# A fused windowed-attention and gated feed-forward kernel: wo loaded in three row parts, the third half's attention placed over its whole stage, cross-pair sums in two operations each

## The chip, the cores and the metric

The kernel runs on one core of a Trainium2 chip. The metric is device time in microseconds. One execution was also taken by the hardware profiler; its page and trace are the source of every duration below. Engine names are those of the profile: PE is TensorE, PEld its weight loads, DVE VectorE, ACT ScalarE, POOL GpSimd and SP the engine that only issues DMAs; POOL and ACT issue DMAs as well. L607 means line 607 of the kernel before.

## What is computed

The inputs are q, k and v of 4 batches, 8 heads, 768 positions and 64 elements per head, and three weight matrices. Attention sees, for each query, the first 8 positions and the 96 positions up to its own, with a bias that falls with distance at a slope of each head's own. The heads side by side make 3072 tokens of 512 elements, which a gated feed-forward layer takes to 1536 and back.

```python
is_global = pos[None, :] < n_global            # 8
is_local  = (rel >= 0) & (rel < n_local)       # 96
scores = q @ k.T / sqrt(D) - slopes * dist     # dist = n_local for far globals
a = softmax(where(is_global | is_local, scores, -1e9))
x = (a @ v) with heads side by side            # 3072 x 512
out = (relu(x @ w_gate) * (x @ w_val)) @ w_out
```

## The kernel before, in words

**Halves and stages.** The work is cut into 8 halves of 384 queries, numbered s = 0 to 7: half s is the first or the second half of the positions of batch s // 2. Each half gets attention (scores, exponentials, a multiplication by a mask, the product with v, division by the sums) and then, under the same number c, the feed-forward layer. TensorE works on the layer of half c while the attention of half c + 1 is placed between its matmuls, and while POOL and SP prepare the keys and queries of half c + 2. The order on each engine is the order in which the program emits instructions; `weave` (L682) emits a list of feed-forward blocks and puts other pieces behind the block at which their share of the list, between 0 and 1, is reached. `spread(items, first, last)` (L677) gives pieces evenly spaced shares.

**The feed-forward layer.** `ffn_pieces` (L598) makes, for each of 12 blocks of 128 hidden rows, a gate block and a value block of four 128x384 matmuls each (L607). ScalarE takes relu of the gate (L614), VectorE multiplies it with the value into `ht` (L620). PSUM has three banks for these ("ff") and five for attention ("x"), so the third block after a given one needs its bank back. Then come the output products with `wo_sb`: plain ones (`outp`, L622, four parts of three row blocks each, L627), or in pairs of 128 tokens by a scheme with seven half-width products instead of eight (`winograd`, L512, matmuls L549), which needs sums of `ht` (`add`, L529 to L535, VectorE) and sums of quarters of `wo_sb` (`wo_sum`, L828, VectorE). From half 4 on, the third 128 tokens of two neighbouring halves make such a pair too; its sums (`add3` in the change, buffers "sums3") run in the stages of halves 5 and 7, behind value blocks 1, 6 and 7, on all six row blocks at once. Results leave through `osb` tiles: copies on ScalarE (L566, L578, L581, L584), additions on VectorE (L569, L574, L588, L589), and DMAs on SP.

**Attention of halves 2 to 7.** `attention_pieces` (L493) gives, for each of four pairs of heads, three score pieces (eight matmuls L397 into four x banks, exponentials L406 on ScalarE, masks L359 on VectorE), two products with v (L427, logarithms of the sums L436 and the exponential that inverts them, L441, on ScalarE), and a norm (L446, VectorE). Empty pieces, two each time for half 2, one for the others, space them.

**Keys and queries.** Loads on SP (L113) bring them in, POOL casts them (`piece_cast`, L361, eight per half), SP transposes them by three DMA transposes (`piece_x`, L367), and `piece_order` (L372) copies the keys of each pair into order, three copies per pair: on POOL, and for pairs 2 and 3 of half 2 on ScalarE.

**The stage that the change touches most** is the last of three `weave` calls for halves 0 and 1: the last 4 hidden blocks of each (16 gate and value blocks), then plain products of half 0 (12 blocks) and the outputs of half 1 (11 blocks), 39 blocks in all, with the attention of half 2, the preparation of half 3 and the sums of `wo_sb` placed into it. Before it POOL has been given, in this order: the load of `wo_sb` (L155, one DMA of all 12 row blocks, in `loads`, L798), fills, the loads of v for half 2, the casts of half 2, with a one-element copy `held` ahead of the last cast that reads the last row block of `wo_sb` and so makes POOL wait for it, two key copies, and the loads for half 3.

Of the kernel before, what the change touches and what calls it, by code (L numbers as in the profile page):

```python
# [15 lines left out]
def kernel(  # L16
# [12 lines left out]
    nc = tc.nc  # L29
# [4 lines left out]
    DM = H * D  # L34
    DFF = moe_w_gate.shape[1]
    N_DC = DM // 128
    N_FC = DFF // 128
# [58 lines left out]
    wo_sb = const.tile([128, N_FC, DM], BF16)  # L96
# [3 lines left out]
    def w_of(t, dc, fc):  # L100
        f = fc % GW
        return t[fc // GW][:, dc, f * 128 : (f + 1) * 128]
# [15 lines left out]
    def v_dst(b, r0, r1, j):  # L118
        t = vbuf[b % 2][r0:r1, j, D:]
        return t.rearrange("p (h z) -> p h z", z=2 * D)[:, :, 0:D]  # L120
# [5 lines left out]
    def spread_v_globals(b, j0=1, j1=NT):  # L126
        if b == 0:
            for j in range(j0, j1):
                nc.sync.dma_start(out=v_dst(b, 0, NG, j), in_=v_dst(b, 0, NG, 0))
        else:  # L130
            t = vbuf[b % 2]
            nc.sync.dma_start(out=t[0:NG, j0:j1, :], in_=t[0:NG, 0:1, :].to_broadcast(
                [NG, j1 - j0, (2 * H + 1) * D]))
# [19 lines left out]

    def load_w(dst, src, f0, f1):
        nc.gpsimd.dma_start(out=dst, in_=src[:, f0:f1].rearrange("(c p) f -> p c f", p=128))  # L155

    def load_w_group(i):
        load_w(wg[i], moe_w_gate, i * GW * 128, (i + 1) * GW * 128)
        load_w(wv[i], moe_w_val, i * GW * 128, (i + 1) * GW * 128)
# [201 lines left out]
    def piece_cast(s, p, i):  # L361
        of = (ks_of, qs_of)[i]
        nc.gpsimd.tensor_copy(  # L363
            kqc[:, :, i].rearrange("t n (h d) -> t h n d", d=D)[:, 2 * p : 2 * p + 2],
            of[s][:, 2 * p : 2 * p + 2, :].rearrange("t e (n d) -> t e n d", n=NN))

    def piece_x(s, n):  # L367
        nc.sync.dma_start_transpose(
            out=kqT[s % 2].rearrange("d i p t -> d (i p) t")[:, :, n * 128 : (n + 1) * 128],
            in_=kqc[:, n].rearrange("t i z -> t (i z)"))  # L370

    def piece_order(s, p):  # L372
        b, half = divmod(s, 2)
        copy = nc.scalar.copy if s == 2 and p >= 2 else nc.gpsimd.tensor_copy
        put_keys(copy, copy, kT[b % 2][p], kNb[s % 2][:, p], half)

    def early_pieces(s):
        out = [(0.0, lambda p=p, i=i: piece_cast(s, p, i)) for i in range(2) for p in range(HP)]
        out += [(0.0, lambda n=n: piece_x(s, n)) for n in range(NN)]
        out += [(0.0, lambda p=p: piece_order(s, p)) for p in range(HP)]  # L380
        return out
# [111 lines left out]
    def attention_pieces(s):  # L493
        QK = lambda p: [(0.15, lambda g=g: piece_qk(s, p, g)) for g in range(3)]
        AV = lambda p: [(0.29, lambda e=e: piece_av(s, p, e)) for e in range(2)]
        N = lambda p: [(0.0, lambda: piece_norm(s, p))]
        g = QK(3)
        a = AV(2)
        gap = [(0.0, lambda: None)] * (2 if s == 2 else 1)
        return (QK(0) + QK(1) + AV(0) + N(0) + gap + QK(2) + AV(1) + N(1) + gap  # L500
                + g[0:1] + a[0:1] + g[1:2] + a[1:2] + g[2:3] + N(2) + AV(3) + N(3))

# [95 lines left out]
    def ffn_pieces(c):  # L598
        ht = ht_pool.tile([128, N_FC, QH], BF16, name="ht")
        st = {}  # L600

        def product(w, key, fc, d0, d1):
            key = key, fc
            if d0 == 0 and key not in st:
                st[key] = psum["ff"].tile([128, 512], FP32, name="ff_ps")
            for dc in range(d0, d1):
                nc.tensor.matmul(st[key][:, 0:QH], lhsT=w_of(w, dc, fc), rhs=xT_of[c][:, dc, :],  # L607
                                 start=(dc == 0), stop=(dc == N_DC - 1))

        def gate(fc, d0=0):  # L610
            product(wg, "g", fc, d0, N_DC)
            psg = st["g", fc]
            gr = gr_pool.tile([128, QH], BF16, name="grelu")
            nc.scalar.activation(gr, psg[:, 0:QH], AF.Relu, bias=0.0, scale=1.0)  # L614
            st["gr", fc] = gr

        def val(fc, d0=0):
            product(wv, "v", fc, d0, N_DC)
            psv = st["v", fc]
            nc.vector.tensor_tensor(ht[:, fc, :], psv[:, 0:QH], st["gr", fc], op=ALU.mult)  # L620

        def outp(n, part):  # L622
            if part == 0:
                st["o"] = psum["ff"].tile([128, 512], FP32, name="ff_ps")
            ps2 = st["o"]
            for fc in range(part * N_FC // 4, (part + 1) * N_FC // 4):
                nc.tensor.matmul(ps2, lhsT=ht[:, fc, n * 128 : (n + 1) * 128],  # L627
                                 rhs=wo_sb[:, fc, :],
                                 start=(fc == 0), stop=(fc == N_FC - 1))
            if part == 3:  # L630
                osb = late["osb"].tile([128, DM], FP32, name="osb")
                nc.scalar.copy(osb, ps2)
                nc.sync.dma_start(out=out_v[c, n], in_=osb)

        def begin():
            two = psum["s"].tile([128, 2, 512], FP32, name="s_ps")
            st["g", 1], st["v", 1] = two[:, 0], two[:, 1]
            for d0, d1 in ((0, 2), (2, N_DC - 1)):
                for key, w in (("g", wg), ("v", wv)):
                    for fc in range(2):  # L640
                        product(w, key, fc, d0, d1)

        plain = range(NN) if c < 1 else () if c - c % 2 in PAIRED else (NN - 1,)
        add, products = winograd([(c, ht, 0), (c, ht, 1)], "sums", (1, 5, 6, 4, 7, 2, 3) if c == NHALF - 1 else
                                 (1, 2, 5, 6, 4, 3, 7) if c in PAIRED else (1, 5, 4, 6, 2, 3, 7))
        behind = {2: [lambda: add(3, 0, 3)], 7 if c == 2 else 5: [lambda: add(3, 3, 6)], 8: [lambda: add(1, 0, 3)],
                  9: [lambda: add(2, 0, 3)], 10: [lambda: add(4, 0, 3)]}
        rest = tuple(lambda j=j: add(j, 3, 6) for j in (1, 2, 4))
        if c in PAIRED:
            third_of[c] = ht  # L650
        elif c - 1 in PAIRED:
            add3, products3 = winograd([(c, ht, NN - 1), (c - 1, third_of[c - 1], NN - 1)], "sums3",
                                       (1, 5, 4, 6, 2, 3, 7))
            behind.update({1: [lambda: add3(1)], 6: [lambda: add3(2)], 7: [lambda: add3(3)]})
            rest = (lambda: add3(4),) + rest

        def val_and_sums(fc):
            val(fc)
            for f in behind.get(fc, ()):
                f()  # L660

        begin_of[c] = (begin, lambda fc=0: gate(fc, N_DC - 1), lambda fc=0: val(fc, N_DC - 1))
        f1 = []
        for fc in range(N_FC):
            f1.append((0.65, lambda fc=fc: gate(fc)))
            f1.append((0.65, lambda fc=fc: (val if c < 1 else val_and_sums)(fc)))
        f2 = [(0.65, lambda n=n, part=part: outp(n, part))
              for n in plain for part in range(4)]
        if c >= 1:
            f2 += (products3 if c - 1 in PAIRED else []) + products  # L670
            places = (2, 3, 5) if plain else (0, 1, 2) if c in PAIRED else (0, 1, 2, 3)
            for at, f in list(zip(places, rest))[::-1]:
                f2.insert(at, (0.0, f))
        return f1, f2


    def spread(items, first, last):  # L677

        n = len(items)
        return [(first + (i + 0.5) / n * (last - first), f) for i, (_, f) in enumerate(items)]  # L680
# [116 lines left out]

    def loads():  # L798
        load_w_group(2)
        load_w(wo_sb, moe_w_out, 0, DM)  # L800
        Z()

    more = {"K0": lambda: load_qk_after(2), "S20": loads}
# [1 line left out]
    for f in ("m0 g0 g1 v0 m3 K3 m2 g2 m1 v1 K2 v2 S30 K0 S31 K1 S21 g3 S20 v3 S01 A3 N3 S00 S11 "  # L805
              "g6 g7 A2 S10 g4 v7 A0 N2 v4 v6 A1 N0 N1 g5 v5").split():
        i = int(f[1])
# [34 lines left out]
    E = [f for _, f in early_pieces(2)]  # L842
    casts, xs, order_k = E[0:8], E[8:11], E[11:15]
    held = rc_pool.tile([1, 1], BF16, name="held")
    for f in (*casts[:7], lambda: nc.gpsimd.tensor_copy(held, wo_sb[0:1, N_FC - 1, 0:1]),
              casts[7], *xs, lambda: spread_v_globals(1), *order_k[:2]):
        f()
    load_qk_after(3, nc.gpsimd)
    load_v_half(3)
    weave(f1_1[G[0]])  # L850
    weave(f1_1[G[1]], [(0.1 + 0.12 * j, lambda j=j: fill_ones(nc.vector, 0, j)) for j in range(NT)])
    weave(f1_0[G[2]] + f1_1[G[2]] + f2_0 + f2_1,
          [(0.33, order_k[2]), (0.38, order_k[3])],
          spread(attention_pieces(2), 0.375, 0.925), spread(early_pieces(3), 0.58, 0.88),
          spread([(0.0, lambda j=j, part=part: wo_sum(j, part)) for j in (1, 3, 2, 4) for part in range(2)],
                 0.1, 0.74))

    ahead = {}
    for c in range(2, NHALF):
# [53 lines left out]
```

## Time and profile before

| | |
|---|---|
| median of three runs | 240.01 us (239.62 to 240.66) |
| profiled execution | 240.08 us, of which 238.3 are the span from the first instruction to the last |
| clock granted to TensorE | 1.0 over the whole span |
| matmuls, gate and value (L607) | 768 of 128x384 in all, 326 ns each as recorded |
| half-width products (L549) | 324 of 128x256, 272 to 273 ns each as recorded |
| plain products (L627) | 68 of 128x512, 379 ns each |
| relu (L614), ht (L620) | 491 ns, 555 ns |
| sums of ht (L535), 384 and 768 wide | 370 to 374 ns, 546 to 627 ns |
| load of wo_sb | one DMA of 1536 KB, 19.0 us from issue to landing |
| DMA transposes | 18 on SP |

A row of the profile gives the line, the engine, the operation, what it writes and reads, how often, the busy time and the mean duration. Recorded durations of matmuls overlap, so a full TensorE shows in the distance between starts. What stands in brackets behind an instruction in the timeline is the idle time of its engine just before it and what ended that.

### The profile page before, as it was taken

The numbers are of one execution on the slowest core, as the hardware profiler recorded it, in microseconds if no ns is written. First come the engines' busy times: TensorE is split into PE (matmuls) and PEld (weight loads), VectorE is DVE, ScalarE is ACT, GpSimd is POOL, SyncE is SP. The second block draws the span as 40 slices with busy tenths as digits, with TensorE's granted clock in tenths as the row PEclk, the third lists the DMA queues.
The fourth block names the chain that finished last, engine by engine and source line by source line (L and its number), as shares of the span: only waits on it lengthen the run. The fifth ranks groups of instructions, "written<-read, shape, count | busy, mean of one in ns | idle before, by whom it ended". The sixth has DMA issues, their size and how long they took to land.

```text
span 238.3 us, 5431 instructions
## 1 busy us (share of the span) xinstructions
PE 231.7 (97%) x1977; PEld 150.1 (63%) x1981; DVE 171.8 (72%) x456; ACT 156.1 (66%) x358; POOL 89.5 (38%) x204
## 2 busy tenths in 40 slices
PE   7899999999999999999999999999999999999994
PEld 3655565655557566666667666856588666766683
DVE  7775965768756778666787677868985786955752
ACT  5896983438767777757777678557686578634330
POOL 6795897007433860903275042723350000000000
PEclk9999999999999999999999999999999999999999
DMA  6999999993996897098519955198432200020022
GB/s 208 183 170 174 241 263 213 191 162 47 286 205 124 260 194 135 10 183 259 101 33 111 236 155 111 25 157 249 78 59 88 90 1 0 4 88 0 3 80 97
DMA packets 70515, 31.42 MB, mean 132 GB/s; under 512 B 47176, under 2 KB 67400, under 8 KB 70488
## 3 DMA queue, kind: packets, MB, share of 16 engines
q0 software_dynamic: 32800, 8.71, 36.0%
q1 hardware_dynamic: 36472, 21.45, 34.3%
q10 hardware_dynamic: 1216, 0.92, 1.2%
q8 instruction: 15, 0.25, 0.4%
q14 instruction: 12, 0.10, 0.1%
HBM read 28.41 MB, written 6.29 MB: 146 GB/s over the span
## 4 chain that ended last, share of the span: by engine, by line
PE 86%; DMA 7%; DVE 2%; POOL 1%; ACT 1%; issue 1%; DVEq 0%
PE ff_ps L607 50%; PE ff_ps L549 12%; DMA wg<-in_moe_w_gate_dram 7%; PE ff_ps L627 7%; PE x_ps L427 6%; PE x_ps L549 5%; PE x_ps L397 4%; PE t_ps L700 1%; PE t_ps L459 1%; POOL kq L737 1%; PE t_ps L272 1%; DVE es L359 0%; DVE ht L620 0%; ACT lnd L436 0%; DVE osb L574 0%
## 5 line engine op out<-in xcount | busy, mean ns | idle before, releaser
L607 PE MATMUL ff_ps<-xT,wg 128*128 128x384 bf16 x380 | 77.7, 326 | 0.4 <-DMA wg<-in_moe_w_gate_dram 0.2
L607 PE MATMUL ff_ps<-xT,wv 128*128 128x384 bf16 x380 | 77.6, 326 | 0.2 <-DVE osb L574 0.2
L614 ACT ACTIVATE grelu<-ff_ps 128x384 bf16<-128x384 f32 x95 | 46.5, 491 | 45.1 <-PE ff_ps L607 23.2
L620 DVE TENSOR_TENSOR ht<-ff_ps,grelu 128x384 bf16<-128x384 f32 x95 | 52.7, 555 | 30.2 <-PE ff_ps L607 19.1
L607 PEld LDWEIGHTS <-wg 128*128 128x128 bf16 x384 | 36.1, 98 | 23.6 <-issue 1.0
L607 PEld LDWEIGHTS <-wv 128*128 128x128 bf16 x384 | 35.8, 98 | 23.3 <-issue 0.5
L406 ACT ACTIVATE es<-x_ps 128x360 bf16<-128x360 f32 (+2 forms) x96 | 35.6, 447 | 3.2 <-PE x_ps L397 3.2
L359 DVE TENSOR_TENSOR es<-es,m_all 128x432 bf16<-128x432 bf16 (+4 forms) x108 | 29.7, 325 | 6.0 <-ACT es L406 5.8
L446 DVE TENSOR_TENSOR xT<-x_ps,rcp 64x384 bf16<-64x384 f32 x48 | 26.6, 554 | 9.2 <-ACT rcp L441 8.4
L436 ACT ACTIVATE lnd<-x_ps 64x384 f32<-64x384 f32 x48 | 23.3, 485 | 10.9 <-PE x_ps L427 10.2
L363 POOL CAST kqc<-ks 128x384 bf16<-128x384 f32 x24 | 12.1, 554 | 31.7 <-DMA ks<-in_k_dram 31.7
L549 PEld LDWEIGHTS <-s 128*128 128x128 bf16 x216 | 21.1, 98 | 2.9 <-issue 0.4
L549 PE MATMUL ff_ps<-t,s 128*128 128x256 bf16 x162 | 21.6, 272 | 0.3 <-ACT osb L584 0.3
L427 PE MATMUL x_ps<-es,vbuf 128*128 128x216 bf16 (+4 forms) x216 | 21.8, 225 | 0.0
L137 POOL DMA_DIRECT2D vbuf<-in_v_dram x25 | 21.6, 881 | 0.3 <-DVE s L535 0.3
L427 PEld LDWEIGHTS <-vbuf 128*128 128x128 bf16 x216 | 15.8, 97 | 6.8
L627 PE MATMUL ff_ps<-wo_sb,ht 128*128 128x512 bf16 x68 | 17.6, 379 | 0.2
L549 PEld LDWEIGHTS <-ht 128*128 128x128 bf16 x162 | 15.5, 98 | 2.3
L263 POOL COPY kT<-kqT 128x240 bf16<-128x240 bf16 x16 | 7.1, 442 | 22.2 <-DMA kqT<-kqc 19.2
L363 POOL CAST kqc<-qs 128x384 bf16<-128x384 f32 x24 | 12.1, 541 | 6.2 <-DMA qs<-in_q_dram 6.2
L535 DVE TENSOR_TENSOR s<-ht 128x384 bf16<-128x384 bf16 (+1 forms) x32 | 12.5, 392 | 0.8
L441 ACT ACTIVATE rcp<-lnd 128x384 f32<-128x384 f32 x24 | 12.6, 524 | 0.8
(118 smaller groups left out, 247.0 us busy)
## 6 DMA issues: line engine op xcount, KB each, us to landing
out_dram<-osb SPq DMA_DIRECT2D x23, 256.0 KB, 2.4
ks<-in_k_dram SPq DMA_DIRECT2D x6, 768.0 KB, 6.2
qs<-in_q_dram SPq DMA_DIRECT2D x6, 768.0 KB, 11.5
vbuf<-in_v_dram POOLq DMA_DIRECT2D x21, 120.0 KB, 7.7
wo_sb<-in_moe_w_out_dram POOLq DMA_DIRECT2D x1, 1536.0 KB, 19.0
wg<-in_moe_w_gate_dram POOLq DMA_DIRECT2D x2, 512.0 KB, 9.8
wv<-in_moe_w_val_dram POOLq DMA_DIRECT2D x2, 512.0 KB, 11.0
wg<-in_moe_w_gate_dram POOLq DMA_DIRECT2D x2, 256.0 KB, 5.8
```

The source lines that it names most:

```text
L137: nc.gpsimd.dma_start(out=v_dst(b, NG + r0, NG + r0 + n, j), in_=v[b, :, KT * j + r0 : KT * j + r0 + n, :].rearrange("h p d -> p h d"))
L359: nc.vector.tensor_mul(for_all, for_all, mk)
L363: nc.gpsimd.tensor_copy(kqc[:, :, i].rearrange("t n (h d) -> t h n d", d=D)[:, 2 * p : 2 * p + 2], of[s][:, 2 * p : 2 * p + 2, :].rearrang ...
L406: nc.scalar.activation(es[:, e, 0:c], banks[e][:, 0:c], AF.Exp, bias=0.0, scale=scale)
L427: nc.tensor.matmul(av3[:, :, a : a + w], lhsT=vb[:, j, z0 : z0 + 128], rhs=es[:, e, c : c + NN * w].rearrange("k (n p) -> k n p", n=NN), s ...
L436: nc.scalar.activation(ln[o0 : o0 + 64], av[d0 : d0 + 64, 0:QH], AF.Ln, bias=0.0, scale=1.0)
L446: nc.vector.tensor_tensor(xT_of[s][r, p, :], av_of[s, p, e][r, 0:QH], av_of[s, p, "r"][r], op=ALU.mult)
L549: nc.tensor.matmul(st[key][:, 0:D2], lhsT=left(i), rhs=right(i), start=start and i == 0, stop=i == N2 - 1, skip_group_check=not start)
L607: nc.tensor.matmul(st[key][:, 0:QH], lhsT=w_of(w, dc, fc), rhs=xT_of[c][:, dc, :], start=(dc == 0), stop=(dc == N_DC - 1))
L614: nc.scalar.activation(gr, psg[:, 0:QH], AF.Relu, bias=0.0, scale=1.0)
L620: nc.vector.tensor_tensor(ht[:, fc, :], psv[:, 0:QH], st["gr", fc], op=ALU.mult)
L627: nc.tensor.matmul(ps2, lhsT=ht[:, fc, n * 128 : (n + 1) * 128], rhs=wo_sb[:, fc, :], start=(fc == 0), stop=(fc == N_FC - 1))
```

## The change

- `wo_sb` is loaded in three DMAs of four row blocks each. The first takes the old place. The second and the third are issued on POOL behind the key copies of pairs 0 and 1 of half 2, so behind that half's transposes; `held` follows them instead of standing ahead of the last cast.
- Half 2's attention is placed from 0.125 to 0.88 of its stage, before from 0.375 to 0.925, with one empty piece each time instead of two; the key copies of pairs 2 and 3 go from 0.33 and 0.38 to 0.2 and 0.25, the sums of `wo_sb` from 0.1 to 0.74 to 0.36 to 0.76.
- In the stages of halves 5 and 7, the second and third cross-pair sums are made in two operations of three row blocks each, behind value blocks 3 and 6, and 4 and 7.

```diff
+    def load_wo(i):
+        f = N_FC // 3
+        nc.gpsimd.dma_start(out=wo_sb[:, i * f : (i + 1) * f], in_=moe_w_out[i * f * 128 : (i + 1) * f * 128].rearrange(
+            "(c p) f -> p c f", p=128))
...
-        gap = [(0.0, lambda: None)] * (2 if s == 2 else 1)
+        gap = [(0.0, lambda: None)]
...
-            behind.update({1: [lambda: add3(1)], 6: [lambda: add3(2)], 7: [lambda: add3(3)]})
+            behind[1] = [lambda: add3(1)]
+            for fc, j, i in ((3, 2, 0), (4, 3, 0), (6, 2, 3), (7, 3, 3)):
+                behind[fc] = [lambda j=j, i=i: add3(j, i, i + 3)]
...
-        load_w(wo_sb, moe_w_out, 0, DM)
+        load_wo(0)
...
-    for f in (*casts[:7], lambda: nc.gpsimd.tensor_copy(held, wo_sb[0:1, N_FC - 1, 0:1]),
-              casts[7], *xs, lambda: spread_v_globals(1), *order_k[:2]):
+    for f in (*casts, *xs, lambda: spread_v_globals(1), order_k[0], lambda: load_wo(1), order_k[1],
+              lambda: load_wo(2), lambda: nc.gpsimd.tensor_copy(held, wo_sb[0:1, N_FC - 1, 0:1])):
         f()
...
-          [(0.33, order_k[2]), (0.38, order_k[3])],
-          spread(attention_pieces(2), 0.375, 0.925), spread(early_pieces(3), 0.58, 0.88),
+          [(0.2, order_k[2]), (0.25, order_k[3])],
+          spread(attention_pieces(2), 0.125, 0.88), spread(early_pieces(3), 0.58, 0.88),
           spread([(0.0, lambda j=j, part=part: wo_sum(j, part)) for j in (1, 3, 2, 4) for part in range(2)],
-                 0.1, 0.74))
+                 0.36, 0.76))
```

## The prediction

> **What bounds the kernel now.** I read the page first, then the waits, then the timeline around each place where TensorE stood still.
>
> The page's busy shares and its chain:
>
> ```profile
> PE 231.7 (97%) x1977; PEld 150.1 (63%) x1981; DVE 171.8 (72%) x456; ACT 156.1 (66%) x358; POOL 89.5 (38%) x204
> ...
> PE 86%; DMA 7%; DVE 2%; POOL 1%; ACT 1%; issue 1%; DVEq 0%
> ```
>
> TensorE sets the end. The change removes no matmul, so it can win only TensorE idle time. Busy time hides small holes, because matmuls overlap; I took them from start times: four 384-column matmuls occupy 0.65 us (gate starts 46.26, value starts 46.91), six 256-column ones 0.655. The waits name who ended the three holes after 28 us that the change can reach:
>
> ```profile
> PE ff_ps L549 <- ACT osb L584: 0.3, 1, 0.3
> PE ff_ps L607 <- DVE osb L574: 0.2, 1, 0.2
> PE ff_ps L607 <- DVE ht L620: 0.2, 1, 0.2
> ```
>
> The first two stand at the end of the third half's stage:
>
> ```profile
> 74.77 0.52 ACT L441 ACTIVATE rcp<-lnd 128x384 f32<-128x384 f32 x1
> 75.20 0.35 ACT L584 COPY osb<-ff_ps 128x256 f32<-128x256 f32 x1
> 75.33 1.14 DVE L446 TENSOR_TENSOR xT<-x_ps,rcp 64x384 bf16<-64x384 f32 x2 [1.24 <-ACT rcp L441]
> 75.60 0.81 PE L549 MATMUL ff_ps<-t,s 128*128 128x256 bf16 x6 [0.26 <-ACT osb L584]
> ...
> 76.84 0.41 DVE L574 TENSOR_TENSOR osb<-ff_ps,osb 128x256 f32<-128x256 f32 x1
> ...
> 77.31 0.81 PE L607 MATMUL ff_ps<-xT,wv 128*128 128x384 bf16 x4 [0.24 <-DVE osb L574]
> ```
>
> The product block before 75.60 started at 74.53, so the next was due at 75.18: 0.42 lost behind the copy L584, which queued on ScalarE behind the last pair's logarithms and rcp. The gate block started at 76.25, the next was due at 76.90 and came at 77.31: 0.41 lost behind L574, itself behind the last pair's norms. The third hole is in piece 5's stage:
>
> ```profile
> 167.52 0.71 DVE L535 TENSOR_TENSOR s<-s,ht 128x768 bf16<-128x768 bf16 x1
> 168.15 1.59 DVE L359 TENSOR_TENSOR es<-es,m_all 128x432 bf16<-128x432 bf16 x4
> 169.66 0.55 DVE L620 TENSOR_TENSOR ht<-ff_ps,grelu 128x384 bf16<-128x384 f32 x1
> ...
> 170.26 0.81 PE L607 MATMUL ff_ps<-xT,wg 128*128 128x384 bf16 x4 [0.17 <-DVE ht L620]
> ```
>
> The block before began at 169.27, so 169.92 was due: 0.34 lost behind a 768-wide sum and four masks. Together 1.17 us, 0.49% of 240.08: the most that this change can win.
>
> **The change, part by part.** Sums are against the profiled run, 240.08 us (span 238.3 and 1.8 around it); the median is 240.01, 0.07 lower.
>
> *Cross-pair sums in halves.* One 768-wide sum behind value 6 and one behind value 7 become 384-wide halves behind values 3, 4, 6, 7. In the chain above the sum occupied VectorE 0.63 (167.52 to 168.15); a half takes 0.37, so ht comes about 0.27 earlier and 0.07 of the hole stays. The half behind value 3 falls into an idle 0.83 before the ht of 163.96. That behind value 4 moves the next ht from 165.72 to 166.09, done 166.65; its PSUM bank is wanted three blocks later, at 166.77: 0.12 to spare. Ends: -0.34 (hole gone) to +0.3 (that spare gone). I take -0.25, by the chain. In piece 7's stage no attention runs and no hole is near.
>
> *Attention from 0.125 instead of 0.375, to 0.88 instead of 0.925.* The stage has 39 blocks, so the first scores move from behind block 16 to behind block 6 (0.1395 x 39 = 5.4), the last pair's second attention product from behind block 35 to 33, its norm from 36 to 34. The three copies that the seventh product waits for then find ScalarE free: lnd 0.49, rcp 0.52 and four copies of 0.35 are 2.4 us, the seventh product comes 3.5 us after block 33. Both holes, -0.83, go; by nothing if another queue is late there (ends -0.83 and 0). What is late next is the front of the stage.
>
> *Keys in time.* The transposes now follow the eighth cast directly, without held, the POOL copy that waits for wo:
>
> ```profile
> 47.47 0.18 POOL L845 COPY held<-wo_sb 1x1 bf16<-1x1 bf16 x1 [5.83 <-DMA wo_sb<-in_moe_w_out_dram]
> ...
> 48.12 4.84 SPq L368 DMA_TRANSPOSE kqT<-kqc  x3
> ...
> 54.92 0.63 POOL L259 COPY kT<-kqT 128x360 bf16<-128x360 bf16 x1 [6.83 <-DMA kqT<-kqc]
> ```
>
> Casts end at 42.1 (41.6 plus 0.5), the transposes take 6.8 (48.12 to 54.92; 5.9 to 6.9 in later halves): 49.0. The three POOL copies of pair 0 take 1.28 (54.92 to 56.20): keys at 50.3. Block 6 ends at 46.26 + 6 x 0.65 = 50.16, plus 0.1 to turn to scores: 50.26. I take 0.1 of wait; ends 0 and 1.0 (four v loads land beside the transposes in both kernels). The spread of v's globals follows them on SP at 47 instead of 53; it is read from 55.7. Behind pair 0's copies POOL issues the second wo part (0.75, as a 512 KB weight group), pair 1's copies (1.31), the third part, and held: pair 1's keys at 52.4, wanted at 52.8.
>
> *ScalarE at the front.* In order it now has relu 0.40, two exps 0.52, relu, two exps 0.70, pair 2's key copies 0.71, relu, two exps, pair 3's copies 0.71, two exps, relu (start-to-start values from 55.3 to 60.2 and 79 to 82). Added from the first exps at 50.6, pair 1's relu behind block 9 starts at 53.3 instead of 52.8, block 11's at 55.63 and ends at 56.12. Its bank is wanted by block 14, due at 55.93: 0.23 of wait, after which relu is level again. Ends: 0, and 0.84 if durations end to end are added instead of starts.
>
> *wo in thirds.* The first part lands where 0.52 MB of the 1.57 do: 39.6 (wv) + 7.8/3 = 42.2. The second is issued at 50.3, the third at 52.4. Nearest rows: v's first load, 384 KB, 5.7 us with a queue empty before it; wo itself 7.8 us for three parts behind others, 2.6 a part. So 56.0 and, 2.6 behind it, 58.6. TensorE wants row block 4 at 59.5 and row block 8 at 60.6 (later than now by the added scores): no wait, ends 0 and the rival below. held ends at 58.7; behind it wait, on POOL, the fourth half's v loads and casts, and on SP its key and query loads, then the out stores, the first wanted near 61. Those loads started at 57.5 and now would at 58.8. Its keys came at 76.28 (POOL copies from 75.47) and would come at 77.6; the first scores, at 78.71 before, would want them at 78.2. Covered, with 0.6 us left. The wo sums on VectorE (eight of 0.55 to 0.89) keep their number and move to 0.36 to 0.76, into blocks with few ht; they end at block 29, the first product that reads them is block 34.
>
> Sum: -0.83 - 0.25 + 0.10 + 0.23 = -0.75, 239.33; on the median 239.3.
>
> A rule of the Trainium skill speaks against moving the wo issues between the key copies: SBUF — State Buffer, section "SBUF: two separate sides", says that a VectorE instruction in a two-port mode locks GpSimd out, so that descriptors of GpSimd's DMAs are not written meanwhile. What the trace has on it is in the third rival.
>
> **The rivals.**
>
> 1. *All holes close and nothing new waits:* 240.08 - 1.17 + 0.1 = 239.0, 238.9 on the median. For: covers are short by tenths only. Against: the ScalarE queue above.
> 2. *Keys late and ScalarE behind:* transposes 1.0 later, beside v's loads, and 0.84 on ScalarE: 239.33 - 0.33 + 1.0 + 0.84 = 240.8. For: the first transpose's issue alone varied from 1.24 to 2.10. Against: as many v loads ran beside them before.
> 3. *POOL stretched by VectorE:* POOL's L260 copy took 0.53 beside VectorE work where its median is 0.20, 2.6 times. An issue of 0.75 would take 1.95, pair 1's keys would come at 53.6, 0.8 late: 240.1. Against: in 20 to 30 us, with VectorE 90% busy, issues took 0.75 to 0.79. By the page's own figures (0.62 us alone, 3.1 beside VectorE) I estimate 2.5 us of wait, 241.8.
> 4. *The third wo part lands late, slower:* the weight groups took 9.8 and 11.0 us from issue. Then the parts land at 60.1 and 63.4; TensorE waits 2.8 at row block 8, and held, 4.8 later than summed, brings the fourth half's keys at 82.4, 4.2 after they are wanted, the 2.8 within that: 243.5. From 59.2 on each us of landing costs one; at 60.0 the gain is gone, from 61.2 it is over 0.5% slower. Against: those groups queued behind others; here the queue has been empty since about 46.
> 5. *The change doesn't do what it says:* the last pair comes earlier, but wo sums and norms now crowd VectorE and the holes return: 240.1.
>
> **How the numbers follow.** About 0.5%, 1.2 us, is what a measurement of this kernel can tell from no change. Forecast 239.3, chance 0.42, own range 238.9 to 240.0. Rivals: 0.20 (three quarters of it over the line, with the run-to-run spread), 0.13 (0.04 slower), 0.05 (0.02), 0.13 (all slower), 0.07 (0.01). Faster 0.15, slower 0.20, same 0.65. The range reaches from rival 1 less 0.3 of spread, 238.6, to 241.8, which holds rival 2 and the milder part of rival 4.
>
> **What would show it.** Right: no TensorE wait on L584 or L574 near 75 us; scores of the third half near 50.3; held near 58; the half sums in piece 5's stage at 0.37 and no wait at 170. Wrong: TensorE waiting on POOL's kT near 50 or 52.5, on ScalarE's relu near 56, on wo near 60, or on kT near 78. A gain over 1.2 us would mean that TensorE lost time that start times do not show; a loss of 2 us or more, a late wo.

## The result, and the profile after

| | kernel before | changed kernel |
|---|---|---|
| median | 240.11 us (239.36 to 241.66, 22 runs) | 242.72 us (239.62 to 245.12, 22 runs) |
| profiled execution | 240.08 us, span 238.3 | 244.50 us, span 242.7 |
| mean granted clock of that execution | 1.0 | 0.993 |

The ratio is 1.0063, 95% interval 1.0036 to 1.009: the change makes the kernel slower. That ratio leaves out executions more than 1.5% above a kernel's fastest, which here are 8 of the changed kernel's 22, among them the profiled one, whose length comes from its own waits, so it understates the loss; the medians differ by 1.1%.

In the changed kernel L612 is the gate and value matmul, L402 the scores, L264 to L266 the key copies on POOL (L268 to L270 for the second half of a batch), L373 the transposes, L368 the casts, L159 the wo loads, L854 `held`, L540 the sums. The page's busy shares and its chain, answering those of before:

```profile
PE 232.5 (96%) x1981; PEld 149.8 (62%) x1981; DVE 172.7 (71%) x460; ACT 156.5 (64%) x358; POOL 90.0 (37%) x206
...
PE 82%; DMA 14%; POOL 1%; SPq 1%; DVE 0%; issue 0%; ACT 0%; POOLq 0%
```

Of the chain that ended last, 14% is now DMA instead of 7%. The waits (engine, instruction, what released it: us in total, times, longest) no longer have the osb and ht rows. They have these, those of the program's first 20 us left out:

```profile
PE x_ps L402 <- POOL kT L266: 2.9, 1, 2.9
...
PE ff_ps L612 <- DMA wg<-in_moe_w_gate_dram: 0.7, 1, 0.7
...
PE ff_ps L612 <- DMA wv<-in_moe_w_val_dram: 0.3, 1, 0.3
```

TensorE waits for the third half's keys. The timeline (start, us, engine, line, instruction; in brackets the idle time before it and what ended that) shows where they were late:

```profile
44.38 2.02 POOL L368 CAST kqc<-qs 128x384 bf16<-128x384 f32 x4 [5.32 <-DMA qs<-in_q_dram]
46.43 4.99 SPq L373 DMA_TRANSPOSE kqT<-kqc  x3
53.43 0.53 POOL L264 COPY kT<-kqT 128x360 bf16<-128x360 bf16 x1 [7.02 <-DMA kqT<-kqc]
54.34 0.45 PE L402 MATMUL x_ps<-kqT,kT 64*128 64x216 bf16 x8 [2.86 <-POOL kT L266]
```

The transposes take 7.0 from issue to the first key copy, as predicted. But they are issued at 46.43 and not at 42.1, because the third half's queries landed at 44.33; in the profiled execution of before they landed at 40.05:

```profile
40.10 1.53 POOL L363 CAST kqc<-qs 128x384 bf16<-128x384 f32 x3 [1.56 <-DMA qs<-in_q_dram]
```

A table by stretches of time (length, then busy us of PE, PEld, DVE, ACT and POOL with counts, granted clock, DMA share, GB/s) has the second cost:

```profile
51.30:54.40 3.10, 0.24 (x4) 0.07 (x4) 0.56 (x1) 0.06 (x1) 0.97 (x4) 1.00 0.65 113
54.40:55.60 1.20, 1.20 (x14) 0.73 (x15) 0.28 (x1) 0.66 (x3) 1.20 (x3) 0.98 0.25 29
55.60:58.90 3.30, 3.30 (x18) 1.35 (x17) 1.44 (x5) 2.79 (x10) 1.25 (x3) 0.50 0.95 145
```

1.2 us after the wait the granted clock falls to 0.50, for 3.4 us in all (55.55 to 58.97): TensorE is busy throughout and does half the work.

**The balance of this execution,** from the distances between matmul starts, against before: up to 50 us +1.2 (most of it two waits for weight groups, 0.7 and 0.3); the wait for keys +2.9; the half clock behind it +1.6; the holes that the change was to close -1.2. Sum +4.5, and the spans differ by 242.7 - 238.3 = 4.4. The +1.2 is not the change's: up to there both kernels issue the same loads, and a variant with the loads of before (tail_only, below) lost 1.65 at the same instruction.

**A second profile of the same changed kernel** (run after_again) had its queries at 39.27, near the 40.05 on which the prediction rests:

```profile
41.34 5.30 SPq L373 DMA_TRANSPOSE kqT<-kqc  x3
48.66 0.54 POOL L264 COPY kT<-kqT 128x360 bf16<-128x360 bf16 x1 [7.34 <-DMA kqT<-kqc]
51.64 0.77 POOL L159 DMA_DIRECT2D wo_sb<-in_moe_w_out_dram  x1 [0.50 <-issue]
59.86 0.53 POOL L854 COPY held<-wo_sb 1x1 bf16<-1x1 bf16 x1 [7.45 <-DMA wo_sb<-in_moe_w_out_dram]
60.48 0.38 SPq L113 DMA_DIRECT2D ks<-in_k_dram  x1
...
77.03 0.81 PE L612 MATMUL ff_ps<-xT,wg 128*128 128x384 bf16 x4
78.52 0.74 PE L402 MATMUL x_ps<-kqT,kT 64*128 64x216 bf16 x10 [0.68 <-POOL kT L268]
```

No wait for keys in the 50s, no half clock. But the third wo part, issued at 51.64, landed at 59.81, `held` let go at 60.4, the fourth half's keys were loaded at 60.48, and its first scores, due at 77.77 (0.74 behind the gate block at 77.03, as in before, 77.97 to 78.71), came at 78.52: 0.75, and 0.26 more inside them. The change's gain near 75, 0.83, is given back three microseconds later. This execution took 239.88 against a median of 239.91 of the kernel before beside it.

The mean granted clock of an execution shows such a stretch without a trace. A stretch of about 3.4 us at half clock takes 1.7 of 242.7, so the mean falls to 0.993, and with two stretches to 0.986. Of the 22 executions of the changed kernel 10 have 0.993 or less, all of them at 242.4 or above; of 81 executions of the kernel before, taken beside the experiments, none is below 0.997. The reverse does not hold: five others of the 22, at 242.33 to 244.77, have a clock of 0.998 or more. None of these was profiled, so where they lost their time is not shown.

### The profile page after: what moved, and what is told of

The parts are those of the page before. It is cut to its first block, busy times and chain, and to the rows that moved or that the text cites. A ratio compares the mean times of both kernels' runs of the same rounds, so it can differ in the third digit from the quotient of the medians.

```text
span 242.7 us, 5438 instructions
## 1 busy us (share of the span) xinstructions
PE 232.5 (96%) x1981; PEld 149.8 (62%) x1981; DVE 172.7 (71%) x460; ACT 156.5 (64%) x358; POOL 90.0 (37%) x206
## 4 chain that ended last, share of the span: by engine, by line
PE 82%; DMA 14%; POOL 1%; SPq 1%; DVE 0%; issue 0%; ACT 0%; POOLq 0%
PE ff_ps L612 44%; PE ff_ps L554 12%; DMA qs<-in_q_dram 8%; PE ff_ps L632 6%; PE x_ps L432 6%; PE x_ps L554 5%; PE x_ps L402 4%; DMA v<-in_v_dram 3%; DMA kqT<-kqc 2%; DMA kq<-in_k_dram 1%; PE t_ps L315 1%; SPq L373 1%; POOL kqc L368 1%; PE t_ps L464 1%; PE t_ps L277 1%; PE s_ps L612 1%
## 5 line engine op out<-in xcount | busy, mean ns | idle before, releaser
L612 PE MATMUL ff_ps<-xT,wg 128*128 128x384 bf16 x380 | 78.4, 329 | 0.7 <-DMA wg<-in_moe_w_gate_dram 0.7
L612 PE MATMUL ff_ps<-xT,wv 128*128 128x384 bf16 x380 | 78.3, 329 | 0.3 <-DMA wv<-in_moe_w_val_dram 0.3
L612 PEld LDWEIGHTS <-wg 128*128 128x128 bf16 x384 | 36.2, 98 | 24.0 <-issue 1.2
L612 PEld LDWEIGHTS <-wv 128*128 128x128 bf16 x384 | 35.8, 98 | 23.7 <-DMA wv<-in_moe_w_val_dram 0.7
L368 POOL CAST kqc<-ks 128x384 bf16<-128x384 f32 x24 | 12.0, 537 | 30.2 <-DMA ks<-in_k_dram 29.6
L368 POOL CAST kqc<-qs 128x384 bf16<-128x384 f32 x24 | 12.3, 553 | 8.3 <-DMA qs<-in_q_dram 8.3
L268 POOL COPY kT<-kqT 128x240 bf16<-128x240 bf16 x16 | 7.3, 454 | 19.6 <-DMA kqT<-kqc 17.9
L402 PE MATMUL x_ps<-kqT,kT 64*128 64x216 bf16 (+4 forms) x216 | 11.3, 227 | 2.9 <-POOL kT L266 2.9
L540 DVE TENSOR_TENSOR s<-ht 128x384 bf16<-128x384 bf16 (+1 forms) x34 | 13.5, 396 | 0.8
## 6 DMA issues: line engine op xcount, KB each, us to landing
wv<-in_moe_w_val_dram POOLq DMA_DIRECT2D x2, 512.0 KB, 11.7
```

Of the source, the lines that this page charges most:

```text
L368: nc.gpsimd.tensor_copy(kqc[:, :, i].rearrange("t n (h d) -> t h n d", d=D)[:, 2 * p : 2 * p + 2], of[s][:, 2 * p : 2 * p + 2, :].rearrang ...
```

## The experiments

The first two theories were A, that only the first keys are late, for lack of cover, so that later attention wins back the holes; and B, that moving the preparation earlier puts the transposes into the weights' traffic and lengthens them. Each expectation says what the theories that it names give. C is that the added work on VectorE and POOL costs the time; sums_only, which adds the four VectorE operations, is not slower. B does not hold for the changed kernel, whose transposes took 7.0 and 7.3 us, but for casts_first. E, that the holes near 75 close only because TensorE has stood still before, is refuted by end_086. The runs led to D: one chain, queries, casts, transposes, pair 0's keys, second wo part, pair 1's keys, third wo part, `held`, fourth half's loads, fourth half's keys, in which no link has cover left, and the links from the wo parts on come later than before (the third part landed at 59.8 and 64.7, before all of wo at 47.4).

**sums_only.** The kernel before with the half-width sums alone.

```diff
-            behind.update({1: [lambda: add3(1)], 6: [lambda: add3(2)], 7: [lambda: add3(3)]})
+            behind[1] = [lambda: add3(1)]
+            for fc, j, i in ((3, 2, 0), (4, 3, 0), (6, 2, 3), (7, 3, 3)):
+                behind[fc] = [lambda j=j, i=i: add3(j, i, i + 3)]
```

> The kernel before with one part of the change: the second and third cross-pair sums in halves. Theory A (the change loses its time where the third half's scores wait for pair 0's keys, because its queries land late beside the weight loads, and wins it at the three holes): the hole of 0.34 near 170 us closes, nothing else moves, 239.8 us, ratio 0.9985 to 0.999. Theory B (the transposes themselves are late beside v's loads): the same here. Theory C (the added work on VectorE and POOL costs the time): slower than before by some tenths, from four more VectorE operations.

Measured: 239.83 against 239.93, ratio 1.0006 (0.9982 to 1.003). The time is A's, its reason is not: the hole near 170 was 0.28 of the former 0.34. The half sum freed 0.37 us on VectorE (0.26 from its start to the masks', before 0.63), but the four masks behind it took 1.90, before 1.59. These masks (L359) follow POOL's casts of the queries, in before

```profile
166.86 2.34 POOL L363 CAST kqc<-qs 128x384 bf16<-128x384 f32 x4 [0.44 <-DMA qs<-in_q_dram]
```

beside the masks from 168.15 on. Where the casts had ended (end_086, end_090, the changed kernel's first profile) the masks took 0.97 to 0.98 and no hole is left; where the casts still ran beside them for 0.4, 1.0 and 1.7 us (after_again, before, sums_only) they took 1.28, 1.59 and 1.90, and the hole was 0.05, 0.34 and 0.28. So the time at which those casts run decides more of this hole than the length of the sum; that it does so by holding VectorE up is read from these six profiles, not tried by itself. This part neither helps measurably nor does the harm.

**thirds_old_place.** The changed kernel with the attention where it was.

```diff
-        gap = [(0.0, lambda: None)]
+        gap = [(0.0, lambda: None)] * (2 if s == 2 else 1)
...
-          [(0.2, order_k[2]), (0.25, order_k[3])],
-          spread(attention_pieces(2), 0.125, 0.88), spread(early_pieces(3), 0.58, 0.88),
+          [(0.33, order_k[2]), (0.38, order_k[3])],
+          spread(attention_pieces(2), 0.375, 0.925), spread(early_pieces(3), 0.58, 0.88),
```

> The changed kernel with the third half's attention put back to 0.375 to 0.925, its key copies to 0.33 and 0.38, and two empty pieces: wo in thirds and the sums in halves stay. Scores of the third half are due near 56.7 us, 6 us later than in the changed kernel. Theories A and B: no wait for keys, no slow clock, the holes of 0.42 and 0.41 near 75 us are back, 239.8 us, narrow spread. Theory C: the time stays near that of the changed kernel (241.5 to 242.7), with waits on wo near 60 us or on the fourth half's keys near 78 us.

Measured: median 244.92 (239.94 to 246.73, 12 runs), seven of the twelve at 244.36 or above with a granted clock of 0.993 or 0.986, the other five at 240.78 or below (ratio of these five 1.0011, 0.9987 to 1.0035). The profiled execution took 245.49, its queries landed at 43.92, and TensorE waited for wo:

```profile
PE ff_ps L632 <- DMA wo_sb<-in_moe_w_out_dram: 3.5, 2, 3.2
...
63.85 1.86 PE L632 MATMUL ff_ps<-wo_sb,ht 128*128 128x512 bf16 x4 [3.24 <-DMA wo_sb<-in_moe_w_out_dram]
```

The third part, issued at 55.86, landed at 63.81. A is refuted: with the scores as late as before and no wait for keys, wo in thirds behind the key copies costs as much in more than half of the executions.

**start_025.** The changed kernel with the attention from 0.25.

```diff
-          [(0.2, order_k[2]), (0.25, order_k[3])],
-          spread(attention_pieces(2), 0.125, 0.88), spread(early_pieces(3), 0.58, 0.88),
+          [(0.29, order_k[2]), (0.33, order_k[3])],
+          spread(attention_pieces(2), 0.25, 0.88), spread(early_pieces(3), 0.58, 0.88),
```

> The changed kernel with the third half's attention from 0.25 instead of 0.125 (to 0.88 as there), key copies of pairs 2 and 3 at 0.29 and 0.33: the first scores come five blocks later, 3.3 us. Theories A and B: waits of up to 3.3 us for keys vanish, the holes near 75 us stay closed: 239.0 to 239.4 us, ratio 0.996 to 0.998. Theory C: 241 to 242.7 us, as the changed kernel.

Measured: 244.28 (240.07 to 246.76, 12 runs), ratio 1.0077 (1.004 to 1.0114). The expectation of A was missed. In the profiled execution, 240.23 with queries at 38.98, TensorE lost 0.62 for wo near 60 and 0.66 and 0.26 for the fourth half's keys at 78; the third part had taken 8.54 from issue.

**casts_first.** The changed kernel with the third half's casts and transposes issued ahead of the last weight group and the first wo part (the diff leaves out where the lists `casts` and `xs` are now made).

```diff
     def loads():
+        for f in casts:
+            f()
+        for f in xs:
+            f()
         load_w_group(2)
...
-    for f in (*casts, *xs, lambda: spread_v_globals(1), order_k[0], lambda: load_wo(1), order_k[1],
+    for f in (lambda: spread_v_globals(1), order_k[0], lambda: load_wo(1), order_k[1],
```

> The changed kernel with one order on POOL and SP altered: the third half's eight casts and three transposes stand ahead of the last weight group's loads and wo's first part, so nothing on the weights' queue competes with the key and query loads. Theory A: the queries land near 33 us instead of 40 to 44, keys of pair 0 are ready near 45, 5 us before the scores at 50.3 want them: no wait, no slow clock, 238.9 to 239.3 us, spread as narrow as before. Theory B: the transposes now run beside the weight group and take longer than 7 us; keys are late by what they are longer. Theory C: no change, 241.5 to 242.7 us.

Measured: 246.22 (244.0 to 246.82), ratio 1.0257 (1.0223 to 1.0291). With no weights ahead of them the queries landed at 34.05, as A has it. The transposes then shared the DMA engines with what was now behind them, as B has it:

```profile
35.99 10.73 SPq L373 DMA_TRANSPOSE kqT<-kqc  x3
54.21 0.53 POOL L264 COPY kT<-kqT 128x360 bf16<-128x360 bf16 x1 [8.86 <-DMA kqT<-kqc]
```

18.2 us instead of 7, and the scores waited 5.4. The DMA view from 39 to 48 us (queue: packets, MB, share), and that of the kernel before from 52 to 54, where transposes run alone:

```profile
q0 software_dynamic: 1405, 1.41, 91.9%
q1 hardware_dynamic: 1405, 0.35, 29.8%
```

```profile
q1 hardware_dynamic: 1593, 0.40, 107.9%
```

The queues take turns packet by packet, 1405 each. A packet of the loads has 1 KB on average, one of the transposes 250 bytes, so the transposes get a fifth of the bytes: 0.35 MB in 9 us, where alone they move 0.40 MB in 2. The Trainium skill, DMA: Bandwidth & Descriptors, section "SWDGE vs HWDGE vs iDMA", says that GpSimd's and the hardware queues are separate inside each DMA engine, and that the engine serves them in rotation; the equal counts agree.

**whole_no_held.** The changed kernel with wo in one load, as before, and the transposes still not behind it.

```diff
-        load_wo(0)
+        load_w(wo_sb, moe_w_out, 0, DM)
...
-    for f in (*casts, *xs, lambda: spread_v_globals(1), order_k[0], lambda: load_wo(1), order_k[1],
-              lambda: load_wo(2), lambda: nc.gpsimd.tensor_copy(held, wo_sb[0:1, N_FC - 1, 0:1])):
+    for f in (*casts, *xs, lambda: spread_v_globals(1), *order_k[:2],
+              lambda: nc.gpsimd.tensor_copy(held, wo_sb[0:1, N_FC - 1, 0:1])):
```

> The changed kernel with wo in one load at the old place and no copy that holds the transposes back; attention from 0.125. Theory D: no wait on wo; but the transposes now run beside the rest of wo and v's loads and take 10 us or more: keys of pair 0 at 53 to 56 instead of 50.3, so 3 to 6 us of wait and a lower clock behind it: 243 to 247 us. If the transposes were not slowed by such company: keys at 50 to 51, 239.5 us.

Measured: 248.93 (248.47 to 249.03), ratio 1.0373 (1.0356 to 1.0391). Transposes issued at 46.20 delivered at 57.87, 11.7 us, beside the rest of wo and v; the wait was 7.7. That is above what I had expected; in the profiled execution the queries were late too, at 44.14. This is what `held` does in the kernel before: it keeps the transposes out of the wo load.

**early_old_wo.** The kernel before, wo and `held` as they were, with the early attention alone.

```diff
-        gap = [(0.0, lambda: None)] * (2 if s == 2 else 1)
+        gap = [(0.0, lambda: None)]
...
-          [(0.33, order_k[2]), (0.38, order_k[3])],
-          spread(attention_pieces(2), 0.375, 0.925), spread(early_pieces(3), 0.58, 0.88),
+          [(0.2, order_k[2]), (0.25, order_k[3])],
+          spread(attention_pieces(2), 0.125, 0.88), spread(early_pieces(3), 0.58, 0.88),
```

> The kernel before with the change's places for the third half's attention alone (0.125 to 0.88, key copies at 0.2 and 0.25), wo in one load, held ahead of the last cast. Keys of pair 0 are ready at 56.2, the scores want them at 50.3. Theory D: TensorE waits 5.9 us there, runs at a lower granted clock behind it (1.5 to 3 us more), and waits nowhere for wo, which landed at 47.4: 246.5 to 248 us, ratio 1.027 to 1.034. Theory E: the same wait.

Measured: 246.56 (245.9 to 247.02), ratio 1.0277 (1.0255 to 1.0298), as D has it. No wait for wo, and this one for keys, with the clock behind it:

```profile
55.71 0.69 PE L397 MATMUL x_ps<-kqT,kT 64*128 64x216 bf16 x8 [5.90 <-POOL kT L261]
...
56.20:59.60 3.40, 3.40 (x15) 1.55 (x12) 0.90 (x3) 2.33 (x8) 2.70 (x7) 0.50 0.44 121
```

So the parts of the change need each other: the early attention needs the transposes ahead of wo, that needs wo cut up, and the cut wo, with its later parts behind the key copies, costs by itself (thirds_old_place).

**parts_beside.** thirds_old_place with wo's second and third part issued right behind the transposes, instead of behind the key copies.

```diff
-    for f in (*casts, *xs, lambda: spread_v_globals(1), order_k[0], lambda: load_wo(1), order_k[1],
-              lambda: load_wo(2), lambda: nc.gpsimd.tensor_copy(held, wo_sb[0:1, N_FC - 1, 0:1])):
+    for f in (*casts, *xs, lambda: load_wo(1), lambda: load_wo(2), lambda: spread_v_globals(1), *order_k[:2],
+              lambda: nc.gpsimd.tensor_copy(held, wo_sb[0:1, N_FC - 1, 0:1])):
```

> The changed kernel with the attention in the old place (0.375 to 0.925) and the second and third wo part issued right behind the transposes' issue instead of behind the key copies. Theory D, with a transpose packet taking turns with a packet of the weights' queue: wo has landed by about 52 us and no wait on it is left near 60; the transposes take 9 to 12 us instead of 7, keys of pair 0 come at 53 to 57, wanted at 56.7: 240 to 241.5 us, against 244.9 with the parts behind the key copies. If wo's lateness had nothing to do with its place behind the transposes: 244 to 245.

Measured: 239.97 against 239.79, ratio 1.0018 (0.9995 to 1.0041). wo landed at 50.2 and 54.1 and nobody waited for it, but the transposes took longer than I had expected:

```profile
40.59 12.15 SPq L373 DMA_TRANSPOSE kqT<-kqc  x3
56.22 0.53 POOL L264 COPY kT<-kqT 128x360 bf16<-128x360 bf16 x1 [14.14 <-DMA kqT<-kqc]
```

15.6 us, keys in order at 57.1, and the scores waited 0.5. This order loses nothing measurable against before and leaves no room for earlier attention. It differs from thirds_old_place only in where the two parts are issued, so their place behind the key copies is what costs there.

**after_again.** The changed kernel once more, to see an execution with early queries.

> The changed kernel itself, for a second profile and more times. Theory D: if this profile has the queries landed near 39 to 40 us (as six of nine profiles had, the others 42 to 44.3), pair 0's keys come within 0.5 us of 50.3, the third wo part lands about 8 us after its issue, near 60.5, where TensorE wants it, and the three holes are closed: 239.2 to 240.2 us for that execution, granted clock 1.0. If they landed near 44, a wait of 3 us at the first scores and 1.5 us of slow matmuls behind it, 243 to 245. Over all executions the times spread over both.

Measured: 241.92 (239.25 to 243.96, 10 runs) against 239.91, ratio 1.0037 (1.0002 to 1.0073). Its profile is shown above; with queries at 39.27 that execution took 239.88, as expected for early ones.

**end_086, tail_only and end_090** leave wo, `held` and the start of the attention as they were and take its end earlier, with the half-width sums of sums_only: the cheapest way to the holes near 75.

```diff
-        gap = [(0.0, lambda: None)] * (2 if s == 2 else 1)
+        gap = [(0.0, lambda: None)]
...
-          spread(attention_pieces(2), 0.375, 0.925), spread(early_pieces(3), 0.58, 0.88),
+          spread(attention_pieces(2), 0.375, 0.86), spread(early_pieces(3), 0.58, 0.88),
```

> The kernel before with what the change wins and without what it moves: the cross-pair sums in halves and the third half's attention from 0.375 (as before) to 0.86 with one empty piece each time; wo in one load and held ahead of the last cast, as before. Theory D (the changed kernel loses by two things that hang on the end of its transposes, the keys wanted at 50 and the second and third wo parts wanted at 59 to 60; it wins by the early end of the attention): no TensorE wait on an osb copy near 75 us, no new one, 239.1 us against 239.9, ratio 0.9965. Theory E (the holes at 75 close only because TensorE has stood still earlier in the stage, and the other queues caught up meanwhile): the two holes stay, 239.8 us.

Measured: 239.72 against 239.79, ratio 0.9996 (0.9984 to 1.0007). The expected 239.1 was missed. The holes near 75 are gone; two new ones of 0.34 (0.72 to the next block instead of 0.38), at 63.0 and 67.7, stand where scores wait for a bank that a norm (L446) still reads.

tail_only keeps both empty pieces and moves only the last five pieces:

```diff
-          spread(attention_pieces(2), 0.375, 0.925), spread(early_pieces(3), 0.58, 0.88),
+          [(0.375 + 0.55 * (i + 0.5) / 28 if i < 23 else (0.825, 0.835, 0.845, 0.865, 0.885)[i - 23], f)
+           for i, (_, f) in enumerate(attention_pieces(2))], spread(early_pieces(3), 0.58, 0.88),
```

> The kernel before with the sums in halves and only the last five attention pieces of the third half earlier (0.825, 0.835, 0.845, 0.865, 0.885 instead of 0.837 to 0.915); the other 23 stay where they were, two empty pieces each time. Theory D: both holes near 75 us close or nearly so, none opens: 239.1 to 239.3 us, ratio 0.997 to 0.9985. If what opened in the kernel with the end at 0.86 (0.26 twice, scores waiting for a bank that a norm still held) comes from the earlier end itself: 239.7.

Measured: 239.96 against 239.91, ratio 1.0009 (0.9989 to 1.0029). The holes at 75 are gone, and the last pair's attention product, now closer behind its scores, waits 0.8 for its masks (L359) at 74.1. The expectation was missed: I had not counted the masks.

end_090 is end_086 with 0.895 in the place of 0.86.

> As the kernel with the end at 0.86, but 0.895: one empty piece, wider spacing. Theory D: holes near 75 us nearly closed, the waits of scores for a norm's bank near 63 and 68 stay, since the missing empty piece makes them: 239.4 to 239.7 us.

Measured: 239.07 (238.65 to 240.25, 12 runs) against 239.91, ratio 0.9973 (0.9957 to 0.9989): faster than both kernels, and better than I expected. It is the best of three such tries, and was measured in one set of runs. Where before had its two holes, matmul blocks now follow each other every 0.65:

```profile
74.44 0.82 PE L549 MATMUL ff_ps<-wo_sb,s 128*128 128x256 bf16 x6
74.51 0.38 ACT L584 COPY osb<-ff_ps 128x256 f32<-128x256 f32 x1
75.09 0.82 PE L549 MATMUL ff_ps<-t,s 128*128 128x256 bf16 x6
...
75.75 0.81 PE L607 MATMUL ff_ps<-xT,wg 128*128 128x384 bf16 x4
76.39 0.81 PE L607 MATMUL ff_ps<-xT,wv 128*128 128x384 bf16 x4
```

The copy L584 starts at 74.51, before at 75.20. 0.34 at 62.6 and a wait of 0.27 for keys at 56.4 are new, so of the 1.17 that the three holes held, all closed here, 0.56 is won by the trace; the ratio gives 0.65 (0.27% of 239.91).

**What the runs say of the links.** All times are of profiled executions, eight of the thirteen.

| run | queries land | transposes issued | to key copies | wo part 3, issue to landing |
|---|---|---|---|---|
| before | 40.05 | 48.12 | 6.8 | (one load) |
| changed | 44.33 | 46.43 | 7.0 | 8.34 |
| after_again | 39.27 | 41.34 | 7.3 | 8.17 |
| start_025 | 38.98 | 40.92 | 7.9 | 8.54 |
| thirds_old_place | 43.92 | 45.98 | 6.9 | 7.95 |
| parts_beside | 38.65 | 40.59 | 15.6 | beside the transposes |
| whole_no_held | 44.14 | 46.20 | 11.7 | (one load) |
| tail_only | 44.74 | 50.35 | 6.2 | (one load) |

## Why the prediction was wrong

**What bounds the kernel** was read rightly. Both holes near 75 closed in both profiles of the changed kernel, and that at 170 wholly in the first and to 0.05 in after_again (predicted remainder 0.07). The arithmetic of the gain, 1.17 at most, held.

**"Keys in time" failed,** and cost most. Its term had four steps. The 6.8 for the transposes was near (7.0, 7.3), pair 0's copies were shorter (0.85 against 1.28), and the scores were due when predicted (51.42 in the changed profile, 1.16 of it lost before the stage began, so 50.26). Wrong was its first number: "casts end at 42.1", which rests on the queries' landing in one execution of before. They ended at 46.4. 4.3 later casts and 0.2 longer transposes, less 0.4 for shorter copies and 1.16 for later scores, make the wait of 2.9 where 0.1 was summed. The landing is not a fixed time. It lay between 38.4 and 40.4 in seven profiles and between 42.0 and 44.7 in five others (casts_first, with no weights ahead of the queries, left out); of the kernels with wo in one load four are in the first group and three in the second, of those with wo in parts three and two. The kernel before hides this: its last cast waits for `held` until 47.5 anyway, 7 us behind the landing of its own profile. The change took that cover away, and I took the row that had never been on the path for its duration. The stated ends, 0 and 1.0 us of wait, had to be 0 and 3.

**The half clock behind a long wait** was put at nothing: 1.6 us in the profiled execution, about 2 in early_old_wo (4.2 us at 0.50 behind the wait's end).

**"wo in thirds" failed as well,** mildly in size and decisively in effect. Part 2 took 5.7 from issue to landing as predicted. Part 3 was put 2.6 behind it, 6.2 from its issue; it took 7.8 to 8.5 in every kernel that issues it behind pair 1's keys. `held` came at 60.4 instead of 58.7, and "covered, with 0.6 us left" became 0.75 and 0.26 late. This is rival 4's mechanism at the point from which it said the gain is gone, 60.0: the prediction held it for unlikely because the queue had been empty; that was so for part 2 and no longer for part 3.

**Rival 2** named late keys but for another reason, transposes longer beside v's loads. In the two profiles they were 0.2 and 0.5 longer; what counted is that they started later. **Rivals 1 and 5** did not happen either: new waits came, and the holes near 75 stayed closed.

**Rival 3** did not happen. The two wo issues took 0.80 and 0.77 in both profiles, the key copies 0.53 to 0.55, 0.20 to 0.39 and 0.22 to 0.23. By the rule of the Trainium skill that the prediction weighed (SBUF — State Buffer, section "SBUF: two separate sides"), 2.5 us of wait had been estimated, and nothing of the kind is there; but VectorE was busy in only 0.09 of the first issue's 0.80 us in after_again and in 0.43 of the second's 0.77, so the rule was hardly put to the test. POOL stood still for 0.32 and 0.50 us before the second issue, for which the profile names no wait; the cause is not known.

**ScalarE at the front** was right where it could be seen: in after_again the value block at 55.96 came 0.24 late behind relu, predicted 0.23. **The sums in halves** met their number by luck: the sum was priced at 0.37 in halves and the masks behind it at their old 1.59, but beside POOL's casts the halves took 0.39 to 0.64 in the changed kernel, and the hole closed because the masks took 0.98 and 1.28. In sums_only the half was short, the masks 1.90, and 0.28 of the hole stayed.

**What stays open** is why the queries land at 39 to 40 in some executions and at 42 to 45 in others. The four profiles with queries at 43.9 or later have the preceding value-weight group at 31.4 to 32.6 instead of 29.3 to 30.5, the third half's keys at 36.3 to 36.9 instead of 31.7 to 34.1, and a TensorE wait for the gate weights near 28 of 0.7 to 1.65 instead of 0.3 at most. tail_only, with all loads of before, has it too, so it is not made by the change; what delays these loads was not tried. That early and late queries make the spread over all executions is read from the profiled ones; the others carry no landing.

## What to carry to other kernels

A transfer that ends well ahead of another wait has an end time that one profile does not bound: before taking that cover away, look at the same landing in several executions, and keep the late one as an end of the range. Cutting a load into parts and putting the later parts behind other work moves everything that its last part guards; follow that guard to the next stage, since the loss can come back 25 us later. When two holes stand at the end of a stage, move the end of the stage: one number (0.925 to 0.895, with one empty piece and the sums in halves) won 0.27%, and the larger change that also moved the start lost time.

## What the runs showed of the hardware that I had not expected

**A TensorE wait of 2.9 us was enough to halve the granted clock.** It fell 1.2 us after the wait had ended, and in early_old_wo during a wait of 5.9 us, at 53.1, until 59.9. In the traces the times between two changes of the clock are whole multiples of 3.41 us, so stretches of that length can be laid over the execution. In the changed kernel the last one at full clock and the slow one are

```profile
52.14:55.55 3.41, 1.22 (x14) 0.75 (x15) 0.24 (x2) 0.63 (x2) 2.12 (x6) 1.00 0.51 79
55.55:58.97 3.42, 3.42 (x18) 1.46 (x17) 1.49 (x5) 2.89 (x10) 1.30 (x4) 0.50 0.94 144
```

Over the thirteen profiles, the ends of the programs included, the clock fell behind every full-clock stretch in which TensorE was busy for 1.32 us or less, 18 of them (0 to 1.22 in the five profiles in which it fell in mid-program), and behind none with 2.03 us or more (2.19 in tail_only, around a wait of 1.65). The limit lies somewhere between. By these figures a wait of 2.9 us that falls half into one stretch and half into the next would leave the clock alone; no run tried that. The Trainium skill, TensorE: Matmul & The Clock Gate, section "What's actually happening", has the clock halved behind at least one idle window of about 3.4 us, counted in windows that run free. The length of the stretches agrees with such a window, and so do the means of 0.993 and 0.986. A window without any matmul was not needed: 1.22 us of matmuls stood in it here.

**Transposes lose to loads on POOL's queue beside them:** from issue to the first key copy they took 7.3 and 7.9 us beside 0.37 and 0.52 MB of such loads, 11.7 beside 0.64 MB, 15.6 beside 1.58 MB and 18.2 beside 1.91 MB. Beside 0.21 MB or less they took 6.1 to 6.3 us in three profiles and 6.8 to 7.0 in five. Loads do not make that last difference (the changed kernel has 0.01 MB beside its 7.0): in the five, one of the three issues on SP took 2.0 to 2.2 us instead of about 1.3, and a 16 KB packet of the profile's instruction queue (q8) falls into that issue; in the three no such packet does. The 6.8 of the prediction holds one of these.

**A half-megabyte load behind another took 7.8 to 8.5 us, the first one 5.4 to 5.8,** though they were issued 2.1 us apart. In the packets the second ends with about 2 us at 12 to 13 KB per us, a sixteenth of the rate before it: about one packet is under way at a time, of 98 ns as before, where some 20 were. Why was not tried.
